# A linear-attention and two-MoE kernel: attention's stretches at other steps, block 0's input turned on TensorE, masks of five chunks on GpSimd

## The chip, the cores and the metric

One core of one Trainium2 chip. The time is the device time of one launch in microseconds (us), median of the runs; less is better.

## The reference

Three layers run one after the other on 3072 tokens of 384 features, all in f32:

```python
for t in range(S):                       # 4 batches, 8 heads, S = 768, head_dim 48
    state = alpha[:, :, t, :, None] * state + einsum('bhd,bhe->bhde', k[:, :, t], v[:, :, t])
    y[:, :, t] = einsum('bhd,bhde->bhe', q[:, :, t], state)
x = tokens(y)                            # 3072 x 384
x = square(relu(x @ w_in)) @ w_out       # 384 -> 2048 -> 384, f64 weights
logits = x @ w_gate + modality_bias[modality_id]
e = argmax(logits)                       # one of 8 experts per token
out = softmax(logits)[e] * (relu(x @ w1[e]) @ w2[e])   # 384 -> 1024 -> 384
```

## The kernel before

**Attention** is cut into 24 chunks of 128 tokens (u = 0 to 23, two batches in turns). For a chunk, `a_scan` and `a_scan2` form running products of alpha on VectorE (DVE) and scale k and q with them. `a_p` multiplies them on TensorE (PE) into two PSUM tiles pp of 128x512, and VectorE masks each half into the SBUF tile pt with one bitwise and. `a_kt` turns k, and ScalarE (ACT) copies it to kt. `a_y` multiplies v by pt, and the carried state by q, into py; ScalarE copies it to y, and two stores put it into the DRAM tensor yt_d, features by tokens. `a_state` multiplies kt by v and VectorE adds that to the state. `finish(u)` is a_y, a_state and, further on, the loads of chunk u + 2; `group(u)` is finish(u - 1), then a_p, a_kt and a_scale of u.

**The first MoE layer** goes over 12 blocks of 256 tokens (n), two chunks each, and 16 slices of 128 hidden features (f). One pair (n, f) is a step. `a_yload` loads a block's x from yt_d into xf, features by tokens, and `a_x` splits it: xh is x rounded on ScalarE, xl the rest on VectorE. Every product is made of three (high by high, high by low, low by high; `mm3`). A step's layer 1 is nine products of 128x256 into ph. ScalarE (relu into g) and VectorE (times relu again), or ScalarE twice in blocks 0 and 1, make the square; gh and gl are its split. Layer 2 comes three steps later (LAG1), six products of 128x392 into po. After a block's last step, VectorE forms lg, ScalarE copies one half of po to ob and VectorE the other; they free the PSUM for the next block's po.

**Weights.** `convert(f)` makes f32 out of f64 bits: per half, ScalarE's mag (line 276) and three rows on VectorE (279, 280, 281). `split` (259, 260) makes wh and wl. `gate_flip` turns w_out's slice on TensorE into pwt, in the one PSUM tile tagged "y", which py, and in a_p of chunks 4 to 6 the second pp, use too; `gate_columns` multiplies it by the gate's weights (306) and appends the result to wh and wl (307, 308).

**Order.** TensorE's instructions go in the order in which the program issues them. The other engines' queues are ordered when the program is built, and each runs its queue in order, as SP does with the DMAs. The program issues `early()` (chunks 0 to 2, the first weights) and then the list `seq` of steps: block 0 alone for 8 steps (LEAD), then blocks 0 and 1 in turns, 32 steps in all (`two`), then blocks 2 to 11. What else is issued stands in `at[gs]`, ahead of the step's layer 1. For block n, `g0` is its first step, and `GA` says at which of its steps the groups of chunks 2n + 3 and 2n + 4 stand. A group's a_scan is issued 4 steps ahead of it, its a_scan2 2 steps; the next block's a_yload stands at step 12, its a_x at 15. `spread` puts the routing of the block before (r_logits, r_rank, r_table) at the steps of ROUTE: 3, 5, 9, 10 to 14. `keep_warm` issues products of the constant tile delta whose result nobody reads.

**After that** come the experts' slots, which gather tokens by expert, on the same engines; GpSimd (POOL) issues their gathers and scatters.

Of the kernel before, what the change touches and what calls it, by code (L numbers as in the profile page):

```python
# [8 lines left out]
F32 = mybir.dt.float32  # L9
F32R = mybir.dt.float32r  # L10
BF16 = mybir.dt.bfloat16
I32 = mybir.dt.int32
AF = mybir.ActivationFunctionType
ALU = mybir.AluOpType
# [3 lines left out]
B, H, S, D = 4, 8, 768, 48  # L18
N = B * S
DM = H * D  # L20
# [3 lines left out]
C = 128  # L24
NU = N // C
CPB = S // C
HP = H // 2
HR = 112
TB = 256
NB = N // TB  # L30
ND = DM // 128
# [148 lines left out]
def gla_moe_moe2(ctx: ExitStack, tc: tile.TileContext, ain, vin, al_d, wio_d, wg_d, wgt_d, mid_d, mb_d, w12_d, out):  # L180
    nc = tc.nc
    pe, act, dve, pool, sp = nc.tensor, nc.scalar, nc.vector, nc.gpsimd, nc.sync
# [10 lines left out]
    p1 = mkpool("p1", 1)  # L193
    p2 = mkpool("p2", 2)
# [4 lines left out]
    ps2 = mkpool("ps2", 2, space=PSUM)  # L199
    ps1 = mkpool("ps1", 1, space=PSUM)  # L200
# [7 lines left out]
    mask = const.tile([128, C], I32, name="mask")  # L208
# [36 lines left out]
    def load_attn(u):  # L245
        load_al(u)
        load_qkv(u)
# [63 lines left out]
    un = {}  # L311
    xt = {}

    def a_scan(u):
        al, qk, v = attn_in.pop(u)
        q, k = qk[:, 0:HP * C], qk[:, HP * C:]
        ar3 = p2.tile([HR, HP, C + 1], F32, name="ar")
        ar = ar3.rearrange("p g t -> p (g t)")
        mul = dve if u < MULD else pool
        dve.tensor_tensor_scan(out=ar, data0=al[:, 0:HP * (C + 1)], data1=delta.rearrange("p g t -> p (g t)"), initial=0.0, op0=ALU.mult, op1=ALU.add)  # L320
        mul.tensor_tensor(out=k.rearrange("p (g t) -> p g t", g=HP), in0=k.rearrange("p (g t) -> p g t", g=HP), in1=ar3[:, :, 0:C], op=ALU.mult)
        ac = ar3[:, :, C:C + 1]

        inv = d1[:, 1:].rearrange("p (g t) -> p g t", g=HP)[:, :, C:]
        dve.tensor_scalar(out=inv, in0=ac, scalar1=PROD_MIN, scalar2=None, op0=ALU.max)
        dve.reciprocal(out=inv, in_=inv)
        un[u] = dict(q=q, k=k, v=v, ac=ac, al=al, mul=mul)
# [9 lines left out]
    def a_p(u):  # L337
        x = un[u]
        pp = [ps1.tile([128, HP, C], F32, tag=t, name="pp") if u in ATG else ps2.tile([128, HP, C], F32, tag="out" if u == 1 else "P", name="pp") for t in ("ms", "y")]
        for hp in range(HP):  # L340
            for j, (r0, r1) in enumerate(((0, 64), (64, HR))):
                pe.matmul(out=pp[j][:, hp, :], lhsT=x["k"][r0:r1, hp * C:(hp + 1) * C], rhs=x["q"][r0:r1, (HP - 1 - hp) * C:(HP - hp) * C], start=True, stop=True)
        x["pt"] = []
        for j in range(2):
            if u in (1, 3):
                pt = p3.tile([128, 2, XW], F32, tag="ob", name="pt").rearrange("p j d -> p (j d)")[:, 0:HP * C].rearrange("p (g t) -> p g t", g=HP)
            else:
                pt = p1.tile([128, HP, C], F32, tag=f"pt{j}", name="pt")
            dve.tensor_tensor(out=pt.bitcast(I32), in0=pp[j].bitcast(I32), in1=mask[:, None, :].to_broadcast([128, HP, C]), op=ALU.bitwise_and)
            x["pt"].append(pt)  # L350

    def a_kt(u):
        x = un[u]
        pk = ps1.tile([128, HP, HR], F32, tag="ms", name="pk")
        for hp in range(HP):
            pe.transpose(out=pk[:, hp, :], in_=x["k"][:, hp * C:(hp + 1) * C], identity=ident[0:HR, 0:HR])
        kt = p1.tile([128, HP, HR], F32, name="kt")
        act.copy(out=kt, in_=pk)
        x["kt"] = kt
# [6 lines left out]
    def a_state(u):  # L366
        x = un.pop(u)
        c = u // 2 % CPB
        if c == CPB - 1:
            return  # L370
        kv = ps1.tile([HR, HP, D], F32, tag="ms", name="kv")
        for hp in range(HP):
            for r0, r1 in ((0, 64), (64, HR)):
                pe.matmul(out=kv[r0:r1, hp, :], lhsT=x["kt"][:, hp, r0:r1], rhs=x["v"][:, hp, r0:r0 + D], start=True, stop=True)
        t = st_t[u % 2][:, :, 0:D]
        if c:
            dve.tensor_tensor(out=t, in0=t, in1=kv, op=ALU.add)
        else:
            dve.tensor_copy(out=t, in_=kv)

    def a_y(u):
        x = un[u]
        c = u // 2 % CPB

        py = ps1.tile([HR, HP, C], F32, tag="y", name="py")
        if c:
            for hp in range(HP):
                for r0, r1 in ((0, 64), (64, HR)):
                    pe.matmul(out=py[r0:r1, hp, :], lhsT=st_t[u % 2][r0:r1, hp, 0:r1 - r0], rhs=x["q"][r0:r1, (HP - 1 - hp) * C:(HP - hp) * C], start=not hp, stop=False, skip_group_check=True)  # L389
        for hp in range(HP):  # L390
            for j, (r0, r1) in enumerate(((0, 64), (64, HR))):
                pe.matmul(out=py[r0:r1, hp, :], lhsT=x["v"][:, hp, r0:r1], rhs=x["pt"][j][:, hp, :], start=not c and not hp, stop=True, skip_group_check=True)
        y = p1.tile([HR, HP, C], F32, name="y")
        act.copy(out=y, in_=py)
        yd = yt_d.rearrange("(g j e) t -> j e g t", g=HP, j=2)
        for j, (r0, r1) in enumerate(HRNG):
            sp.dma_start(out=yd[j, :, :, u * C:(u + 1) * C], in_=y[r0:r1])

    def a_yload(n):
        x = p1.tile([128, ND, TB], F32, name="xf")  # L400
        sp.dma_start(out=x, in_=yt_d.rearrange("(d p) t -> p d t", p=128)[:, :, n * TB:(n + 1) * TB])
        xt[n] = x

    def a_x(n):
        xh = p2.tile([128, ND, TB], F32R, name="xh")
        xl = p2.tile([128, ND, TB], F32R, name="xl")
        act.copy(out=xh, in_=xt[n])  # L407
        dve.tensor_tensor(out=xl, in0=xt[n], in1=xh, op=ALU.subtract)  # L408
        xt[n] = (xh, xl)

    def transpose_split(y, dst, j, pp, tag):
        px = pp.tile([128, ND, 128], F32, tag=tag, name="px")
        for d in range(ND):
            pe.transpose(out=px[:, d, :], in_=y[:, d * 128:(d + 1) * 128], identity=ident)
        hi, lo = (t[:, :, j * 128:(j + 1) * 128] for t in dst)
        act.copy(out=hi, in_=px)
        dve.tensor_tensor(out=lo, in0=px, in1=hi, op=ALU.subtract)
# [351 lines left out]
    ROUTE0 = 14, 15, 16, 17, 18, 19, 20, 21  # L769
    ROUTE = 3, 5, 9, 10, 11, 12, 13, 14  # L770
    ROUTEZ = 3, 3, 4, 5, 6, 6, 7, 8
    GA = 1, 8
    PRE = 4
    LEAD = 8
    LAG1 = 3
    POOLGL = ()
    WARM = 4
    MULD = NU

    ATG = {4: 12, 5: 18, 6: 24}  # L780
    gq = {}

    if True:
# [15 lines left out]
        def keep_warm(n):  # L799
            warm = ps2.tile([HR, HP * C], F32, tag="h", name="warm")  # L800
            for _ in range(n):
                pe.matmul(out=warm, lhsT=delta[:, 0, 0:HR], rhs=delta.rearrange("p g t -> p (g t)")[:, 0:HP * C], start=True, stop=True)
# [25 lines left out]
        def scan(u):  # L828
            a_scan(u)
            a_scan2(u)  # L830

        def finish(u, load=True):
            a_y(u)
            a_state(u)
            if load and u + 2 < NU:
                load_attn(u + 2)

        def group(u):

            finish(u - 1)  # L840
            if u < NU:
                a_p(u)
                a_kt(u)
                a_scale(u)
# [41 lines left out]
        def put(gs, *steps):  # L886
            at.setdefault(gs, []).extend(steps)

        def early():
            scan(0)  # L890
            a_p(0)
            a_kt(0)
            scan(1)
            finish(0, False)
            a_p(1)
            a_kt(1)
            a_scan(2)
            cv(0)
            a_scan2(2)
            cv(0)  # L900
            cv(0)
            finish(1, False)
            cv(0)
            cv(0)
            cv(1)
            a_yload(0)
            load_attn(3)
            cv(1, 3)
            cv(2)
            a_scale(2)  # L910
            gate_columns(*gate_flip())
            a_p(2)
            a_kt(2)
            a_x(0)

        put(1, lambda: finish(2, False), lambda: load_attn(4), lambda: a_scan(3))
        put(2, lambda: a_scan2(3), lambda: a_scale(3))
# [14 lines left out]
        for n in range(2, NB):  # L932
            g0 = two + (n - 2) * NF
            for i in range(2):
                u = 2 * n + 3 + i
                if u <= NU:
                    put(g0 + GA[i] + 2 * (u == 7), lambda u=u: group(u))
                    if u < NU:
                        put(g0 + GA[i] - 4, lambda u=u: a_scan(u))
                        put(g0 + GA[i] - 2, lambda u=u: a_scan2(u))  # L940
            if n < NB - 1:
                put(g0 + 12, lambda n=n: a_yload(n + 1))
                put(g0 + 15, lambda n=n: a_x(n + 1))
        g0 = two + (NB - 3) * NF
# [10 lines left out]
        for m in range(NB - 1):  # L955
# [7 lines left out]
            g0 = two + (m - 1) * NF  # L963
            spread([g0 + k for k in (ROUTE if 0 < m < NB - 2 else ROUTE0 if m == 0 else ROUTEZ)], route())
        for i in range(NA):
            g0 = two + (3 + i // 2) * NF + 8 * (i % 2)
# [157 lines left out]
```

## Time and profile before

| | |
|---|---|
| median of 3 runs | 825.29 us (824.69 to 828.78) |
| the profiled execution's own time | 822.23 us |
| its span, first to last instruction | 820.4 us |
| TensorE busy | 769.2 us, 94%, 6174 instructions |
| VectorE busy | 543.6 us, 66% |
| ScalarE busy | 402.6 us, 49% |
| GpSimd busy | 64.5 us, 8% |
| granted TensorE clock, mean | 0.974 of 2.4 GHz |
| DMA | 105.39 MB, 128 GB/s over the span |

Busy time is the union of an engine's instructions. A product of f32 tiles is two instructions in attention, and its end is modelled. A row of a timeline has the start in us from the span's start, the duration of the merged instructions, engine, line, operation, the tile written and those read, shapes and count; in brackets stands the idle time of the engine before it and what ended that. A row of waits sums such idle times. A granted clock of 1.00 is 2.4 GHz, 0.50 is 1.2 GHz.

### The profile page before, as it was taken

The numbers are of one execution on the slowest core, as the hardware profiler recorded it, in microseconds if no ns is written. First come the engines' busy times: TensorE is split into PE (matmuls) and PEld (weight loads), VectorE is DVE, ScalarE is ACT, GpSimd is POOL, SyncE is SP. The second block draws the span as 40 slices with busy tenths as digits, with TensorE's granted clock in tenths as the row PEclk, the third lists the DMA queues.
The fourth block names the chain that finished last, engine by engine and source line by source line (L and its number), as shares of the span: only waits on it lengthen the run. The fifth ranks groups of instructions, "written<-read, shape, count | busy, mean of one in ns | idle before, by whom it ended". The sixth has DMA issues, their size and how long they took to land. (4 is left out here: it accounts for less than half of the span.)

```text
span 820.4 us, 16492 instructions
## 1 busy us (share of the span) xinstructions
PE 769.2 (94%) x6174; PEld 738.6 (90%) x6174; DVE 543.6 (66%) x1370; ACT 402.6 (49%) x895; POOL 64.5 (8%) x85
## 2 busy tenths in 40 slices
PE   6589999999999999999999999999899999999992
PEld 4478989999998998999999999999889999999992
DVE  8889985776665664676767554456896666666631
ACT  2467879533333333333333333334666666666631
POOL 1000000000000000000000000002013322223110
PEclk9599999999999999999999999999999999999996
DMA  8877566232313211222222211105878777777600
GB/s 241 232 198 219 173 182 192 63 87 56 90 50 103 62 58 39 81 61 76 63 64 64 64 30 30 30 20 172 248 241 240 237 218 230 227 224 231 194 30 18
DMA packets 56019, 105.39 MB, mean 128 GB/s; under 512 B 9163, under 2 KB 29141, under 8 KB 55920
## 3 DMA queue, kind: packets, MB, share of 16 engines
q1 hardware_dynamic: 52720, 94.49, 39.2%
q0 software_dynamic: 3200, 9.65, 3.4%
q8 instruction: 53, 0.87, 0.5%
q14 instruction: 46, 0.38, 0.2%
HBM read 89.95 MB, written 14.36 MB: 127 GB/s over the span
## 5 line engine op out<-in xcount | busy, mean ns | idle before, releaser
L430 PE MATMUL ph<-xh,wh 128*128 128x256 f32 x864 | 249.7, 289 | 7.9 <-ACT xh L407 4.8
L430 PE MATMUL ph<-xl,wh 128*128 128x256 f32 x864 | 243.0, 281 | 1.5 <-DVE xl L408 1.5
L430 PE MATMUL ph<-xh,wl 128*128 128x256 f32 x864 | 243.0, 281 | 0.0
L430 PE MATMUL po<-wh,gh 128*128 128x392 f32 (+1 forms) x584 | 201.6, 345 | 9.4 <-ACT ob L874 5.7
L430 PE MATMUL po<-wh,gl 128*128 128x392 f32 (+1 forms) x584 | 198.3, 340 | 0.0
L430 PE MATMUL po<-wl,gh 128*128 128x392 f32 (+1 forms) x584 | 198.2, 339 | 0.0
L430 PEld LDWEIGHTS ph<-xh,wh 128*128 128x128 f32 x864 | 163.5, 189 | 10.9 <-ACT xh L407 5.1
L430 PEld LDWEIGHTS ph<-xl,wh 128*128 128x128 f32 x864 | 163.8, 190 | 1.8 <-DVE xl L408 1.8
L430 PEld LDWEIGHTS ph<-xh,wl 128*128 128x128 f32 x864 | 163.5, 189 | 0.0
L260 DVE TENSOR_TENSOR wl<-st,wh 128x768 fp32r<-128x768 f32 x104 | 99.5, 957 | 62.5 <-ACT wh L259 62.5
L996 ACT CAST gh<-g 128x256 fp32r<-128x256 f32 x192 | 77.9, 406 | 116.5 <-DVE g L992 116.1
L998 DVE TENSOR_TENSOR gl<-g,gh 128x256 fp32r<-128x256 f32 x192 | 80.8, 421 | 62.3 <-ACT gh L996 61.9
L430 PEld LDWEIGHTS po<-wh,gh 128*128 128x128 f32 x584 | 110.1, 189 | 11.5 <-ACT ob L874 6.9
L985 ACT ACTIVATE g<-ph 128x256 f32<-128x256 f32 x192 | 73.6, 383 | 94.9 <-PE ph L430 94.6
L259 ACT CAST wh<-st 128x768 fp32r<-128x768 f32 x104 | 86.7, 834 | 56.0 <-PE po L430 42.6
L992 DVE SCALAR_TENSOR_TENSOR g<-ph,g 128x256 f32<-128x256 f32 x160 | 67.3, 421 | 66.1 <-ACT g L985 65.7
L430 PEld LDWEIGHTS po<-wl,gh 128*128 128x128 f32 x584 | 110.3, 189 | 0.0
L430 PEld LDWEIGHTS po<-wh,gl 128*128 128x128 f32 x584 | 110.0, 188 | 0.2 <-DVE gl L998 0.2
L727 ACT ACTIVATE gh<-ph 128x256 fp32r<-128x256 f32 x96 | 37.0, 386 | 22.3 <-PE ph L430 20.3
L729 DVE SCALAR_TENSOR_TENSOR gl<-ph,gh 128x256 fp32r<-128x256 f32 x96 | 40.0, 417 | 8.6 <-ACT gh L727 8.5
L563 POOL IOTA row<- 1x96 f32 x1 | 0.2, 234 | 473.7 <-PE py L389 473.7
L745 POOL DMA_INDIRECT out_dram<-xs,ix x25 | 27.3, 1093 | 114.9 <-ACT xs L744 59.6
(187 smaller groups left out, 817.0 us busy)
## 6 DMA issues: line engine op xcount, KB each, us to landing
st<-in_w_dram SPq DMA_DIRECT2D x104, 384.0 KB, 3.9
st<-in_wio_dram SPq DMA_DIRECT2D x32, 384.0 KB, 4.0
qk<-in_ain_dram SPq DMA_DIRECT2D x23, 448.0 KB, 4.2
al<-in_ain_dram SPq DMA_DIRECT2D x24, 226.2 KB, 2.9
v<-in_vin_dram SPq DMA_DIRECT2D x24, 224.0 KB, 3.3
scr<-ob SPq DMA_DIRECT2D x12, 385.0 KB, 3.0
yt_d<-y SPq DMA_DIRECT2D x48, 96.0 KB, 2.8
xf<-yt_d SPq DMA_DIRECT2D x12, 384.0 KB, 3.5
```

Source lines behind the costliest of these rows:

```text
L259: act.copy(out=hi[:, 0:2 * DM], in_=t)
L260: lo_eng.tensor_tensor(out=lo[:, 0:2 * DM], in0=t, in1=hi[:, 0:2 * DM], op=ALU.subtract)
L430: pe.matmul(out=out_, lhsT=lhs[a][lsl], rhs=rhs[b][rsl], start=first and i == 0, stop=last and i == 2)
L563: pool.iota(thr, pattern=[[0, E], [SLOT, NJ]], base=0, channel_multiplier=0, allow_small_or_imprecise_dtypes=True)
L727: act.activation(out=gh[:, cols], in_=h, func=AF.Relu)
L729: dve.scalar_tensor_tensor(out=gl[:, cols], in0=h, scalar=0.0, in1=gh[:, cols], op0=ALU.max, op1=ALU.subtract)
L745: pool.indirect_dma_start(out=out[:, :], out_offset=bass.IndirectOffsetOnAxis(ap=x["ix"][:, 2 + j:3 + j], axis=0), in_=xo[:, 0:DM], in_off ...
L985: act.activation(out=g, in_=ph, func=AF.Relu)
L992: dve.scalar_tensor_tensor(out=g, in0=ph, scalar=0.0, in1=g, op0=ALU.max, op1=ALU.mult)
L996: act.copy(out=gh, in_=g)
L998: (pool if n in POOLGL else dve).tensor_tensor(out=gl, in0=g, in1=gh, op=ALU.subtract)
```

## The change

1. For chunks 2 to 6 (`PSEL`), ScalarE copies each half of pp from PSUM to pt, and GpSimd masks pt in place with an affine select. Chunks 0, 1 and 7 to 23 keep VectorE's mask.
2. Chunks 0 and 1 go through `a_first`: y is formed as tokens by features (eight products of 48 columns into pyt), ScalarE copies it to yt, and after a_state `transpose_split` turns it in three transposes into px and splits px into xh and xl of block 0 directly, 128 tokens each. px is taken from the two-buffer PSUM tag "out", which pp of chunk 1 uses too. The stores of y of these chunks, the load of xf and a_x for block 0 go.
3. `keep_warm` is issued with three products ahead of chunk 0's y and two ahead of chunk 1's, into the PSUM tag "h".
4. The groups stand at steps 3 and 10 of a block instead of 1 and 8 (chunk 7's stood at 3 already). The scans move with them.

```diff
@@ a_p
-            dve.tensor_tensor(out=pt.bitcast(I32), in0=pp[j].bitcast(I32), in1=mask[:, None, :].to_broadcast([128, HP, C]), op=ALU.bitwise_and)
+            if u in PSEL:
+                act.copy(out=pt, in_=pp[j])
+                pool.affine_select(out=pt, in_=pt, compare_op=ALU.is_ge, fill=0.0, base=-127, pattern=[[0, HP], [1, 128]], channel_multiplier=1)
+            else:
+                dve.tensor_tensor(out=pt.bitcast(I32), in0=pp[j].bitcast(I32), in1=mask[:, None, :].to_broadcast([128, HP, C]), op=ALU.bitwise_and)
...
+    def a_first(u):
+
+        x = un[u]
+        py = ps1.tile([128, DM], F32, tag="y", name="pyt")
+        for hp in range(HP):
+            for j in range(2):
+                o = (2 * hp + j) * D
+                pe.matmul(out=py[:, o:o + D], lhsT=x["pt"][j][:, hp, :], rhs=x["v"][:, hp, 64 * j:64 * j + D], start=not o, stop=True, skip_group_check=True)
+        y = p1.tile([128, DM], F32, tag="y", name="yt")
+        act.copy(out=y, in_=py)
+        if 0 not in xt:
+            xt[0] = tuple(p2.tile([128, ND, TB], F32R, name=k) for k in ("xh", "xl"))
+        return lambda: transpose_split(y, xt[0], u, ps2, "out")
...
-    GA = 1, 8
+    GA = 3, 10
...
+    PSEL = range(2, 7)
...
         def finish(u, load=True):
-            a_y(u)
+            turn = a_first(u) if u < 2 else a_y(u)
             a_state(u)
+            if turn:
+                turn()
...
             a_kt(0)
+            keep_warm(3)
             scan(1)
             finish(0, False)
             a_p(1)
             a_kt(1)
+            keep_warm(2)
...
-            a_yload(0)
             load_attn(3)
...
             a_kt(2)
-            a_x(0)
...
-                    put(g0 + GA[i] + 2 * (u == 7), lambda u=u: group(u))
+                    put(g0 + GA[i], lambda u=u: group(u))
```

**How it moves instructions.** A row has the line, the operation, the tile written and those read, the shape written, and a count. The changed kernel's lines are some 4 to 21 higher: 342 stays, 349 is 353, 392 of chunks 0 and 1 is replaced by 410 (pyt), 408 of block 0 by 432 (px) and 435 (xl).

The first place is TensorE between chunk 0's state and chunk 1's y; in brackets stand the engines and queues whose semaphores a row waits for (`DVE_49` is VectorE). Before:

```order
L374 MATMUL kv<-v,kt 48x48
L342 MATMUL pp<-qk 128x128 [waits DMAHW5_49]
L342 MATMUL pp<-qk 128x128 x7
L356 MATMUL pk<-ident,qk 128x112 [waits DVE_49]
L356 MATMUL pk<-ident,qk 128x112 x3
L392 MATMUL py<-pt,v 64x128 [waits DMAHW6_49,DVE_49,Activation_49]
```

Now:

```order
L378 MATMUL kv<-v,kt 48x48
L432 MATMUL px<-ident,yt 128x128 [waits Activation_49]
L432 MATMUL px<-ident,yt 128x128 x2
L342 MATMUL pp<-qk 128x128 [waits DMAHW5_49]
L342 MATMUL pp<-qk 128x128 [waits DVE_49]
L342 MATMUL pp<-qk 128x128 x6
L360 MATMUL pk<-ident,qk 128x112 x4
L821 MATMUL warm<-delta 112x512 x2
L410 MATMUL pyt<-v,pt 128x48 [waits DMAHW6_49,DVE_49]
```

The transposes of chunk 0 stand ahead of chunk 1's pp, whose second product waits for VectorE; two constants' products stand behind pk.

The second place is VectorE from the copy of chunk 0's state to chunk 1's mask. Before:

```order
L379 COPY state_105<-kv 112x4x48
L279 TENSOR_SCALAR w<-mag 128x384
L364 TENSOR_TENSOR state_105<-state_105,ar 112x4x48
L280 SCALAR_TENSOR_TENSOR w<-st,w 128x384
L279 TENSOR_SCALAR w<-mag 128x384
L349 TENSOR_TENSOR pt<-pp,mask 128x512 x2
```

Now:

```order
L279 TENSOR_SCALAR w<-mag 128x384
L280 SCALAR_TENSOR_TENSOR w<-st,w 128x384
L383 COPY state_105<-kv 112x4x48
L281 SCALAR_TENSOR_TENSOR w<-mag,w 128x384
L279 TENSOR_SCALAR w<-mag 128x384 x2
L280 SCALAR_TENSOR_TENSOR w<-st,w 128x384
L435 TENSOR_TENSOR xl<-px,xh 128x3x128
L281 SCALAR_TENSOR_TENSOR w<-mag,w 128x384
L280 SCALAR_TENSOR_TENSOR w<-st,w 128x384
L279 TENSOR_SCALAR w<-mag 128x384
L321 TENSOR_TENSOR qk<-qk,ar 112x512
L353 TENSOR_TENSOR pt<-pp,mask 128x512 x2
```

From the first of these rows on the mask stands behind twelve instructions, among them half of block 0's xl, where it stood behind five.

The third place is ScalarE where the steady block 5 begins, about the copy ob of block 4. Before:

```order
L394 COPY y<-py 112x512
L358 COPY kt<-pk 128x448
L985 ACTIVATE g<-ph 128x256
L996 CAST gh<-g 128x256
L985 ACTIVATE g<-ph 128x256
L996 CAST gh<-g 128x256
L874 COPY ob<-po 128x384
```

Now:

```order
L1017 CAST gh<-g 128x256
L895 COPY ob<-po 128x384
L398 COPY y<-py 112x512
L485 ACTIVATE ex<-sh 128x16
L362 COPY kt<-pk 128x448
L1006 ACTIVATE g<-ph 128x256
```

ob stood two steps behind the group's y and kt; now it stands ahead of y. Behind the second group of a block, xh (407, now 425) comes after y, kt and two pairs of g and gh in both kernels.

## Rows read from the trace of the kernel before

**Rows 1.** Windows: us, busy us (instructions) of PE PEld DVE ACT POOL, clock, DMA
```profile
20.00:43.00 23.00, 13.39 (x95) 11.34 (x92) 20.32 (x41) 9.71 (x20) 0.00 (x0) 0.57 0.76 219
...
64.00:130.00 66.00, 61.63 (x521) 58.50 (x521) 57.62 (x129) 52.53 (x132) 0.00 (x0) 1.00 0.62 189
130.00:440.00 310.00, 301.60 (x2628) 289.08 (x2627) 202.11 (x570) 122.74 (x308) 0.00 (x0) 1.00 0.26 75
```

**Rows 2.** TensorE's waits, whole run: line waited for, us in total, times, longest
```profile
PE po L430 <- ACT ob L874: 5.7, 6, 1.2
PE ph L430 <- ACT xh L407: 4.8, 1, 4.8
PE py L392 <- DVE pt L349: 3.4, 1, 3.4
...
PE ph L430 <- DVE g L992: 2.6, 3, 1.9
...
PE pwt L299 <- DVE pt L349: 2.4, 2, 1.6
...
PE ph L430 <- DVE xl L408: 1.5, 1, 1.5
...
PE pk L356 <- DVE pt L349: 0.5, 1, 0.5
```

**Rows 3.** Timeline of ScalarE, head: start, us, operation, [idle before <-releaser]
```profile
21.55 0.58 ACT L394 COPY y<-py 112x512 f32<-112x512 f32 x1
```

**Rows 4.** Timeline of TensorE, head (an f32 product is two instructions)
```profile
1.59 5.83 PE L802 MATMUL warm<-delta 112*112 112x512 f32 x8 [1.59 <-POOL delta L793]
...
36.48 0.84 PE L299 MATMUL pwt<-ident,w 128*128 128x128 f32 x3
```

**Rows 5.** Timeline of VectorE, head
```profile
16.31 0.33 DVE L379 COPY state<-kv 112x192 f32<-112x192 f32 x1
...
17.83 1.28 DVE L349 TENSOR_TENSOR pt<-pp,mask 128x512 int32<-128x512 int32 x2
...
25.59 0.62 DVE L279 TENSOR_SCALAR w<-mag 128x384 int32<-128x384 int32 x2
...
28.92 1.02 DVE L280 SCALAR_TENSOR_TENSOR w<-st,w 128x384 int32<-128x384 int32 x2
...
45.08 0.96 DVE L260 TENSOR_TENSOR wl<-w,wh 128x768 fp32r<-128x768 f32 x1 [0.15 <-ACT wh L259]
```

**Rows 6.** VectorE's waits from 16 to 60 us
```profile
DVE wl L308 <- ACT wh L307: 2.3, 4, 1.1
DVE state L377 <- PE kv L374: 1.0, 1, 1.0
DVE w L279 <- PE pwt L299: 0.7, 1, 0.7
```

**Rows 7.** Timeline of GpSimd, head
```profile
1.97 0.28 POOL L806 TENSOR_SCALAR_AFFINE_SELECT mkf<-mkf 128x128 f32<-128x128 f32 x1
```

**Rows 8.** Timeline of TensorE at the start and the middle of two blocks
```profile
300.38 1.09 PE L392 MATMUL py<-pt,v 128*64 128x128 f32 x16
...
369.13 1.08 PE L389 MATMUL py<-qk,state 64*64 64x128 f32 x16
...
373.08 0.37 PE L430 MATMUL ph<-xh,wh 128*128 128x256 f32 x1
...
377.42 0.28 PE L430 MATMUL ph<-xh,wh 128*128 128x256 f32 x1
...
379.56 0.44 PE L430 MATMUL po<-wh,gh 128*128 128x392 f32 x1 [0.90 <-ACT ob L874]
```

**Rows 9.** Timeline of the SP queue in the block of 300.38
```profile
307.20 0.38 SPq L401 DMA_DIRECT2D xf<-yt_d  x1
```

**Rows 10.** Timeline of VectorE in the same block
```profile
312.82 0.96 DVE L408 TENSOR_TENSOR xl<-xf,xh 128x768 fp32r<-128x768 f32 x1 [2.06 <-ACT xh L407]
```

**Rows 11.** The tile xf over the run: its loads
```profile
DMA to landing us min/median/max: 3.2/3.5/5.0
```

## The prediction

> **What bounds the kernel now.** I read the stretches first, then who waits for whom, and only then rows in order of time. TensorE is busy nearly throughout, so time is to be had only where it stands idle or runs at its lower clock, and the stretches tell where. From 130 to 440 us, the steady blocks, it is busy for 301.60 of 310 us and idle for 8.4. From 20 to 43 us, before and around the first step, it is busy for 13.39 of 23 us at a granted clock of 0.57, that is mostly at 1.2 GHz. From 64 to 130 us it idles for 4.4 us while VectorE is busy for 57.62 of 66 [rows 1]. The list of TensorE's waits names what ended the idle time: 5.7 us in six pieces for ob (the copy of a finished block's result, which frees its PSUM), 4.8 for xh and 1.5 for xl of block 0, 3.4 for chunk 0's mask [rows 2]. The reader should see that the head has two limits of nearly one height, TensorE's chain and VectorE's queue of weight conversions: what comes off one of them alone is lost to the other.
>
> **Head, TensorE's side.** Block 0's x goes by DRAM now: y of chunk 1 is copied at 21.55 in 0.58 us [rows 3], stored, loaded again and split, and the first step's products end at 36.48 [rows 4]. The change turns y on TensorE: one ScalarE copy, three transposes and two half splits in place of that. The waits for xh and xl go, 4.8 + 1.5 = 6.3 us [rows 2]. On the SP queue four stores and a load go too, and chunk 3's loads no longer stand behind stores that wait for y.
>
> Three things are added or moved. *The constants' products.* Four took 5.83 us at the start [rows 4], 1.46 each, so three take at most 4.4, 1.0 more than the 3.4 us wait for chunk 0's mask that they fill, and less at the upper clock; two lie in the wait for chunk 1's. I book nothing, and up to 1.0 in the lower end. *A new wait.* px of chunk 0 takes one of the two PSUM buffers that chunk 1's pp use, so its second pp product stands until VectorE has made xl from px, behind six conversion rows and the state copy: some 4 us, which pk and py of chunk 1 wait with it. *A moved mask.* Chunk 1's mask began at 17.83, 1.5 us after the state copy at 16.31 [rows 5]. Ahead of it stand now four L279 (two take 0.62), five L280 or L281 (two take 1.02), the state copy of 0.33, a multiply (0.64, as half a mask) and half an xl (0.48, as half a wl) [rows 5]: 1.24 + 2.55 + 1.45 = 5.2 us, so it begins near 21.5, and the new wait is over by then. TensorE therefore comes to step 0 near 28, not much later than it reaches its wait now, and starts it at once: the products end between 28.5 (at 2.4 GHz) and 33 (if it stays at 1.2) instead of 36.48. This chain gains 3.5 to 8 us.
>
> **Head, VectorE's side.** It sets the end here, since each step needs wl of its weights. The fourth step's wl starts at 45.08 [rows 5]. On the way VectorE waits 4.0 us for TensorE's late chain (2.3 behind wh, 1.0 for kv, 0.7 for pwt) [rows 6]; these go if x is early. The masks of chunks 2 and 3 leave it, 1.28 us each [rows 5]. The two half xl cost what the whole one did. That is 6.6 us. Against it I put 1.5 us of new waits of VectorE for kv, px and xh of chunk 1, which TensorE now makes later. **Head: 5 us**, between 1.5 and 8.5.
>
> What hides the masks' new cost: per chunk two ScalarE copies of 0.58, as y's [rows 3], and two GpSimd selections. One of 128x128 took 0.28 [rows 7]; one of 128x512 lies between that and four times it, 1.12. I take 0.85, nearer the upper end since it passes over four times the elements. Chunk 2's pt is then there 2.9 us after pp, while TensorE still has pk, step 0, a turn of gate weights and the state's half of py to do. If ScalarE comes late, py stands, and layer 1 of the next step behind it.
>
> **64 to 130 us.** The gate weights' turn waits 2.4 us for the masks of chunks 4 and 5, whose pp lie in its PSUM bank, and pk 0.5 for chunk 6's [rows 2]. ScalarE's copies free the bank now, behind other ScalarE work and 1.2 us for the pair. I take half, **1.5 us**, with bounds of 0 and 2.9.
>
> **The blocks.** A step takes 2.17 us (two from 373.08 to 377.42), the group of attention ahead of it began at 369.13, so it takes 4.0; then the new block's first layer 2 waits 0.90 for ob at 379.56 [rows 8]. The group stood at step 1 and is over by then. At step 3 it stands between the old block's last layer 2 and the new block's first, and ob is copied under it. **All six waits go, 5.7 us** [rows 2]; the least I would believe is 4. What is late next is y: the second group stands at step 10 instead of 8 and writes the y that the next block loads. In one block that load was issued at 307.20 [rows 9], and xl stood in VectorE's queue for 2.06 us before xh came [rows 10]; TensorE's 1.9 us for g [rows 2] are that case. ScalarE's order keeps xh behind the second relu after the group, as before, so the distance stays and I book nothing more for it.
>
> **Sum.** 5 + 1.5 + 5.7 = 12.2 us. The profiled execution took 822.23 us for a span of 820.4. It lies 3.1 below the median of 825.29, so the sum gives 810 on its time and **813 us** on the median, which I predict. All lower ends (1.5 - 1.0 + 0 + 4) leave 821, all upper ends (8.5 + 2.9 + 5.7, and 1.9 for the late load) 806.
>
> **Rivals.**
> *GpSimd holds VectorE up.* GpSimd's rows before 440 us are its set-up [rows 7], so no row shows it at work beside VectorE's scans and splits: the trace neither bears this out nor excludes it. If every selection stops VectorE for its length, chunks 2 and 3 cost 4 x 0.85 = 3.4 us in the head, and the gain at chunks 4 to 6 goes: 5 - 3.4 + 0 + 5.7 = 7.3, so 818 us. The Trainium skill, "SBUF — State Buffer", section "SBUF: two separate sides", says this of the pair: a GpSimd instruction and a VectorE one that reads two inputs from SBUF exclude each other, and the one that comes second stands for the whole length of the first. Chance 0.15.
> *The waits for ob come back as waits for g.* At step 3 the group's scan, mask and state meet the routing's rows on VectorE; g comes late, and ph with it. Against it: the group crowds VectorE as much at step 1 now, and there are only three waits for g in the whole run [rows 2]. If all 5.7 come back, 6.5 are left: 819 us. Chance 0.08.
> *The x load comes too late in every block, and the kernel is slower.* After a group, 4.0 us, TensorE runs four steps, 8.7, before the layer 1 that needs the PSUM which the g behind xl frees: 12.7. Back from there, g takes 0.4, xl 0.95 and xh about as much, so the load must have landed 10.4 us after the group began. In the row shown it was issued 6.8 us after (300.38 to 307.20 [rows 8, 9]), and loads take 3.2 to 5.0 [rows 11]: 10 to 11.8. Each us beyond is paid in nine blocks. The 12.2 us are eaten where all nine land at 11.8; at 12.7 the stall is 2.3 each, 20.7 in all: 834 us. Against it: one such stall of 1.9 us now, and the order keeps the distance. Chance 0.05.
>
> **How the numbers follow.** Forecast 0.72, the rivals 0.15, 0.08 and 0.05. A measurement of this kernel tells 0.5%, 4.1 us, from no change, so the line is at 821.2. The forecast lies below it but for its farthest end, 818 and 819 do by less than their own spread: faster 0.87, same 0.09, slower 0.04. The range of 805 to 820 holds the forecast, the 818 and the 819, and leaves out the last rival and the far lower end.
>
> **What would show it.** Right: no wait of po for ob; none for xh or xl before step 0, whose products end before 33 us; the fourth wl near 40; GpSimd selections under 1.2 us. Wrong: VectorE rows that stretch while those run; xl standing over 1 us in VectorE's queue in most blocks; py waiting for pt of chunks 2 to 6; conversions waiting for weights, whose transfers run at 219 GB/s in the head already [rows 1].

## The result, and the profile after

The changed kernel takes **815.47 us** (median of 6 runs, 812.33 to 817.51) against 824.99 for the kernel before beside it (6 runs, 822.40 to 828.78): ratio 0.9873, 95% interval 0.9846 to 0.9900. The forecast was 813 us, its range 805 to 820. The profiled execution took 815.84 us for a span of 814.1 at a mean granted clock of 0.976; before it was 822.23 for 820.4 at 0.974.

The stretches of the changed kernel, to be read against [rows 1]: us, then busy us and instructions of PE, PEld, DVE, ACT, POOL, then granted clock, DMA share and GB/s.

```profile
0.00:20.00 20.00, 15.30 (x77) 8.30 (x79) 16.70 (x32) 5.05 (x9) 2.91 (x20) 0.95 0.87 238
20.00:43.00 23.00, 20.07 (x162) 16.44 (x160) 17.37 (x36) 10.93 (x24) 1.62 (x2) 0.74 0.76 207
43.00:60.00 17.00, 13.12 (x93) 12.01 (x92) 14.62 (x31) 12.15 (x30) 1.54 (x2) 0.87 0.71 181
64.00:130.00 66.00, 60.60 (x493) 56.96 (x491) 56.39 (x126) 51.85 (x128) 6.10 (x4) 0.99 0.62 183
130.00:440.00 310.00, 308.70 (x2723) 297.48 (x2718) 211.62 (x591) 129.36 (x324) 1.23 (x2) 1.00 0.27 77
```

In the steady blocks, 130 to 440 us, TensorE is idle for 1.3 us where it was for 8.4. In the head TensorE is busier than before and VectorE less busy (17.37 of 23 us against 20.32): VectorE now stands. From 64 to 130 us TensorE idles for 5.4 us instead of 4.4, so nothing came of the 1.5 us forecast there.

TensorE's waits over the whole run, which answer to [rows 2]:

```profile
PE pwt L306 <- ACT wt L301: 4.3, 6, 1.2
PE pwt L299 <- DVE w L281: 2.9, 3, 1.4
PE pp L342 <- DVE xl L435: 2.6, 1, 2.6
PE pwt L299 <- DVE wl L308: 1.9, 3, 0.7
...
PE ph L448 <- DVE wl L260: 1.4, 2, 1.1
PE ph L448 <- DVE g L1013: 1.3, 2, 0.7
```

The 5.7 us for ob, the 4.8 for xh and the 1.5 for xl of block 0 are gone, the 3.4 for chunk 0's mask fell to 0.5 and the 2.6 for g to 1.3. New is pp for xl, once, 2.6 us (px holds its PSUM buffer). The waits of the gate weights' turn grew: for w from 0.4 to 2.9, for wt from 2.5 to 4.3.

To see which part brought what, I compare the starts of the same instruction in both traces. Chunk 5's y (its first product of q and the state) starts at 125.87 us before and at **129.70** in the changed kernel: up to there the changed kernel is 3.8 us behind in these two executions, where 6.5 of gain were forecast. From there to layer 1 of step 170 (the first is step 0) it takes 389.6 us instead of 399.0: the blocks have won **9.4**, where 5.7 were forecast. So the sum came out near because two errors had opposite signs, and that is luck.

The head's chain on TensorE in the changed kernel, to be read against [rows 4]: start, us, operation, [idle before it <- who ended that].

```profile
15.85 0.55 PE L432 MATMUL px<-ident,yt 128*128 128x128 f32 x3
16.32 0.49 PE L342 MATMUL pp<-qk 64*128 64x128 f32 x2
19.40 2.07 PE L342 MATMUL pp<-qk 48*128 48x128 f32 x14 [2.59 <-DVE xl L435]
21.40 1.01 PE L360 MATMUL pk<-ident,qk 112*128 112x112 f32 x4
22.20 3.24 PE L821 MATMUL warm<-delta 112*112 112x512 f32 x4
25.27 1.88 PE L410 MATMUL pyt<-v,pt 128*128 128x48 f32 x16
...
31.51 0.36 PE L448 MATMUL ph<-xh,wh 128*128 128x256 f32 x1
```

The first step starts at 31.51 instead of near 28. VectorE's side of it, against [rows 5, 6]:

```profile
21.09 1.29 DVE L353 TENSOR_TENSOR pt<-pp,mask 128x512 int32<-128x512 int32 x2
...
27.81 0.36 DVE L383 COPY state<-kv 112x192 f32<-112x192 f32 x1 [3.02 <-PE kv L378]
...
41.00 0.35 DVE L381 TENSOR_TENSOR state<-state,kv 112x192 f32<-112x192 f32 x1 [1.99 <-PE kv L378]
...
45.38 0.96 DVE L260 TENSOR_TENSOR wl<-w,wh 128x768 fp32r<-128x768 f32 x1
```

Chunk 1's mask begins at 21.09, as worked out (21.5). But after it VectorE stands 3.02 and 1.99 us for kv of chunks 1 and 2, and the fourth step's wl starts at 45.38, as late as before (45.08) and not near 40.

### The profile page after: what moved, and what is told of

It reads as the page before. It is cut to its first block, busy times and chain, and to the rows that moved or that the text cites. A ratio compares the mean times of both kernels' runs of the same rounds, so it can differ in the third digit from the quotient of the medians.

```text
span 814.1 us, 16533 instructions
## 1 busy us (share of the span) xinstructions
PE 776.7 (95%) x6190; PEld 742.9 (91%) x6190; DVE 545.3 (67%) x1361; ACT 408.3 (50%) x906; POOL 73.3 (9%) x95
## 5 line engine op out<-in xcount | busy, mean ns | idle before, releaser
L701 POOL DMA_INDIRECT xs<-scr,ix x25 | 28.4, 1137 | 70.5 <-DVE rf L521 21.7
```

The source lines that it names most:

```text
L701: pool.indirect_dma_start(out=xs[:, j, 0:XW], out_offset=None, in_=scr[0:rows, :], in_offset=bass.IndirectOffsetOnAxis(ap=ix[:, j:j + 1], ...
```

## The experiments

The times stand together here. Clock (granted, mean from 0 to 60 us), first step and chunk 5's y are those of each profiled execution, in us.

```
kernel                               median (runs)       ratio to before [95%]   clock  step 0  chunk 5's y
before (first profile)               825.29 (3)                                  0.80   32.52   125.87
changed                              815.47 (6)          0.9873 [0.9846 0.9900]  0.85   31.51   129.70
1 stretches at steps 3, 10 alone     815.28 (6)          0.9870 [0.9843 0.9897]  0.80   32.35   126.01
2 all but the stretches              822.04 (12)         0.9975 [0.9954 0.9996]  0.91   30.75   127.50
3 masks on VectorE                   814.38 (6)          0.9886 [0.9858 0.9915]  0.89   30.46   126.22
4 px in other buffers                811.36 (5)          0.9835 [0.9808 0.9862]  0.97   26.98   121.82
5 no added products                  815.87 (9)          0.9917 [0.9892 0.9942]  0.77   33.31   129.05
6 x by DRAM                          816.85 (6)          0.9917 [0.9888 0.9946]  0.89   31.64   126.68
7 px in other buffers, no products   815.71 (6)          0.9906 [0.9876 0.9935]  0.74   34.04   130.40
8 px in other buffers, masks VectorE 813.28 (6)          0.9889 [0.9854 0.9924]  0.92   27.17   126.62
9 wait for px filled                 811.10 (6)          0.9846 [0.9817 0.9876]  0.97   29.87   123.88
10 as 4, again                       811.98 (6)          0.9836 [0.9806 0.9867]  0.91   29.27   125.02
11 as 8, again                       815.52 (6)          0.9897 [0.9869 0.9924]  0.83   31.60   128.20
```

The kernel before, beside them, took 823.86 (1 to 4), 824.27 (5 to 8) and 823.81 (9 to 11). One kernel's head moves by some 3 us between executions (4 and 10: 121.82 and 125.02), so the medians decide where two traces are that close. The changed kernel ran beside a kernel before of 824.99, about 1 us more; where medians and ratios tell different things of it, both are given.

### 1 and 2. The stretches alone, and all the rest alone

On the kernel before:

```diff
-    GA = 1, 8
+    GA = 3, 10
...
-                    put(g0 + GA[i] + 2 * (u == 7), lambda u=u: group(u))
+                    put(g0 + GA[i], lambda u=u: group(u))
```

> The kernel before with the groups at steps 3 and 10 alone; the head is the old one. Theory A (from the changed kernel's trace: its head is 3.8 us late at chunk 5's y, 129.70 against 125.87, and the blocks win more than that back): the blocks alone bring 8 to 10 us, ratio 0.988 to 0.990, chunk 5's y within 1 us of 125.87, no wait of po for ob. Theory B (the forecast: 5.7 us from the blocks, the rest from the head): 5 to 6.5 us, ratio 0.992 to 0.994.

The other kernel undoes these lines in the changed kernel.

> The changed kernel with the groups back at steps 1 and 8: all of the head's edits and GpSimd's masks, none of the blocks'. Theory A: no gain, 0 to 4 us slower than before (ratio 1.000 to 1.005), chunk 5's y near 129, the six waits for ob back at 5 to 6 us. Theory B: 5 to 6.5 us faster, ratio 0.992 to 0.994.

The stretches alone take 815.28 us, the whole change's time, 8.6 us less than before, as theory A had it (the ratio, 0.9870, is a little under its 0.988), with chunk 5's y at 126.01. Their blocks, from the windows:

```profile
130.00:440.00 310.00, 308.09 (x2686) 297.09 (x2686) 212.91 (x592) 126.19 (x318) 0.00 (x0) 1.00 0.27 76
```

and no wait for ob is left. Without the stretches it stands there as before; this is the first row of TensorE's waits in the second kernel:

```profile
PE po L448 <- ACT ob L895: 5.7, 6, 1.3
```

That kernel's ratio is 0.9975, a gain of 0.3 to 3.8 us. Neither expectation of its time was met: theory A had it 0 to 4 us slower, with chunk 5's y near 129 (it came at 127.50), theory B 5 to 6.5 faster. So the head's three parts together are worth little (2 us alone, nothing measurable beside the stretches), though the waits that they were to take away are gone. The next runs ask which part loses what another gains.

### 3. The masks of chunks 2 to 6 back on VectorE

```diff
-    PSEL = range(2, 7)
+    PSEL = ()
```

> The changed kernel with the masks of chunks 2 to 6 back on VectorE. Theory A with a lock between GpSimd and VectorE (in the changed kernel VectorE rows of usually 0.55 us take 0.89 to 0.99 beside the selections): the masks' move is worth little, so within 2 us of the changed kernel either way, ratio to the kernel before 0.985 to 0.991. Theory B (the masks' 2.5 us on VectorE and 1.5 us of pwt's waits are a gain): 3 to 4 us slower than the changed kernel, ratio 0.991 to 0.993.

814.38 us, within theory A's 2 us of the changed kernel: the masks' move is worth nothing that can be measured here. TensorE's turn of the gate weights waits longer without it (5.1 us for w against 2.9, and 2.0 for masks), and yet chunk 5's y comes 3.5 us earlier in this execution, at a higher clock.

### 4. px in other PSUM buffers

```diff
-        return lambda: transpose_split(y, xt[0], u, ps2, "out")
+        return lambda: transpose_split(y, xt[0], u, ps2, "h")
```

> The changed kernel with px of chunks 0 and 1 in the PSUM tag h instead of out, so that chunk 1's pp needn't wait for VectorE's xl. If that wait (2.6 us) and the late, slow-clocked products behind it (pyt and kv of chunk 1 end at 27.8) are what cost the head its gain, the wait of pp goes, step 0 starts 3 us or more before 31.5, chunk 5's y comes at 126 or earlier, and the time falls by 3 to 5 us against the changed kernel (ratio to before 0.982 to 0.984). If the head's end is set later, by conversions on VectorE from 44 us on, step 0 comes earlier but chunk 5's y stays within 1.5 us of 129.7 and the time within 1.5 us of the changed kernel's.

811.36 us, by the medians 4.1 less than the changed kernel, by the ratios 3.1; the expectation was met in each point. Its chain on TensorE, to be held against that of the changed kernel above:

```profile
15.69 0.55 PE L432 MATMUL px<-ident,yt 128*128 128x128 f32 x3
16.16 1.16 PE L342 MATMUL pp<-qk 64*128 64x128 f32 x16
17.30 0.60 PE L360 MATMUL pk<-ident,qk 112*128 112x112 f32 x4
17.74 1.88 PE L821 MATMUL warm<-delta 112*112 112x512 f32 x4
...
26.98 0.56 PE L448 MATMUL ph<-xh,wh 128*128 128x256 f32 x1
```

From the start of chunk 1's pp to the first step it takes 10.8 us instead of 15.2, 4.4 less, more than the wait of 2.59. The rest is in the durations: pp and pk take 1.14 + 0.44 us here, start to start, and 5.08 - 2.59 + 0.80 in the changed kernel without its wait; the two constants' products 2.10 (a wait of 0.22 for the mask included) against 3.07. Of these gains 0.9 is lost again between y and the first step. So in these two executions the wait cost its length and then the clock. Two things changed at once, though: the products come earlier, and they run faster.

### 5 and 7. Without the added constants' products

```diff
-            keep_warm(3)
...
-            keep_warm(2)
```

once on the changed kernel, once with px in the other buffers.

> The changed kernel without its five added constants' products; all else as changed. In the changed kernel's profile the two before y of chunk 1 stand from 22.20 to 25.27 us, 3.08 at 1.2 GHz, while chunk 1's mask began at 21.09 and takes 1.28: some 2.9 of the 3.08 us lie on the path to the first step. Theory (px's wait for its PSUM buffer cost the head its gain, the products only lengthen it): the 2.6 us wait of pp for xl stays, the first step starts 2 to 3 us earlier than 31.51, chunk 5's y near 128 instead of 129.7, time 812.5 to 815. Rival (the products keep the clock up, and without them it is lower for longer): granted clock from 20 to 43 us under 0.70, the first step no earlier, 816 to 819. Second rival (the products were the whole loss): as fast as the kernel with px in the other buffer, 811.

> The changed kernel with px in the other PSUM buffers and without the five added constants' products. Theory (with px's wait gone the masks' waits are all that the products fill, and they keep the clock up there): first step between 26 and 28 us, the granted clock from 20 to 43 us below the 0.93 of the kernel with the products, time 811 to 814 against 811.4. Rival (the products stand on the path in this version too, 1 to 2 us ahead of each y): first step near 25, 809 to 810.5.

In the changed kernel the products do little for the time: 815.87 without them against 815.47; by the ratios 0.0044, 3.6 us, with intervals that overlap. My theory missed there (first step at 33.31, not 2 to 3 us earlier), and the rival that they keep the clock up came near: a clock of 0.57 from 20 to 43 us, the first step no earlier, a time 0.1 under its range. Without them the wait for px is short, since TensorE is late already:

```profile
12.79 3.82 PE L410 MATMUL pyt<-v,pt 128*128 128x48 f32 x16 [2.93 <-DVE pt L353]
...
19.63 2.07 PE L342 MATMUL pp<-qk 48*128 48x128 f32 x14 [0.44 <-DVE xl L435]
```

Its clock is 0.50 from 12.4 to 36.2 us, so there was no upper clock left that a wait could end.

With px in the other buffers the products do count: 815.71 without, 811.4 and 812.0 with. The first step comes at 34.04 there, and the granted clock from 20 to 43 us is 0.50, that is 1.2 GHz throughout. Of that kernel, TensorE in the head:

```profile
12.86 0.42 PE L410 MATMUL pyt<-v,pt 128*128 128x48 f32 x2 [3.13 <-DVE pt L353]
...
20.99 3.82 PE L410 MATMUL pyt<-v,pt 128*128 128x48 f32 x16
24.74 1.09 PE L378 MATMUL kv<-v,kt 128*64 128x48 f32 x16
```

y takes 3.82 us here and 1.88 in the changed kernel's chain. My expectation, first step at 26 to 28 and 811 to 814 us, missed: the clock stays low for longer than I had thought. So the free buffer brings nothing without the products (815.87 and 815.71), and the products little while px holds the buffer: **each is needed for the other's full worth**. That leaves two readings of the wait: it makes TensorE late, or it undoes what the products are there for.

### 9. The wait for px filled, not removed

On the changed kernel, px in the buffer as changed:

```diff
             finish(0, False)
+            keep_warm(3)
             a_p(1)
```

> The changed kernel, px in the buffer as changed, with three more constants' products on TensorE ahead of chunk 1's pp: they fill the wait for px's PSUM buffer (2.59 us, three products take 2.3 at 2.4 GHz) without taking it away. Theory (the wait costs twice: its own 2.6 us, and the lower clock from 18.1 to 24.9 us that follows the idle time): clock stays up, so pk, the products, y and kv of chunk 1 take 6.6 us less the half that the clock gives back; first step between 28 and 29.8 us instead of 31.51 (26.98 with px in the other buffer), time 812 to 815. Rival (only the lateness counts): first step at 31 to 32, 815 to 817.

811.10 us, all that the other buffer brings by the medians (the ratios, 0.9846 and 0.9873, lie 2.2 us apart and their intervals just touch). The time is under the theory's 812 to 815, and the first step at 29.87, only 1.6 us earlier than in the changed kernel, just misses its 28 to 29.8. Chunk 1's pp still comes late:

```profile
15.79 0.55 PE L432 MATMUL px<-ident,yt 128*128 128x128 f32 x3
16.18 2.74 PE L821 MATMUL warm<-delta 112*112 112x512 f32 x6
18.84 1.65 PE L342 MATMUL pp<-qk 64*128 64x128 f32 x16
20.43 0.60 PE L360 MATMUL pk<-ident,qk 112*128 112x112 f32 x4
20.86 1.88 PE L821 MATMUL warm<-delta 112*112 112x512 f32 x4
```

The stretch from 18.2 to 24.8 us shows what changed: first the changed kernel, then this one.

```profile
18.20:24.80 6.60, 5.40 (x22) 3.55 (x23) 6.59 (x13) 2.13 (x4) 0.00 (x0) 0.50 0.94 258
```

```profile
18.20:24.80 6.60, 5.94 (x37) 3.52 (x35) 6.60 (x14) 2.58 (x5) 0.00 (x0) 1.00 0.88 259
```

The granted clock is 0.50 in the one and 1.00 in the other, and TensorE has 22 instructions in it against 37. The rival, that only the lateness counts (815 to 817 us, first step at 31 to 32), falls. VectorE's 3.02 us for kv fell to 0.8 in this kernel.

Two things limit this. Of the 5.8 us by which chunk 5's y is earlier, 4.2 come behind the first step (the clock from 43 to 60 us is 1.00 against 0.87), and no run shows that they follow from the filled wait. And the clock isn't set by the wait alone: from 18.2 to 24.8 us it is 0.50, 0.74 and 0.74 in the profiles with the wait (changed, 2, 3), 1.00, 1.00, 1.00 and 0.90 in four with the products and that wait gone or filled (4, 8, 9, 10), but 0.50 in experiment 11, which has the products and no wait for px. That the difference isn't of these executions alone is told by the mean granted clock of whole runs: its median is 0.978 for the changed kernel, 0.984 and 0.984 for experiments 4 and 10, 0.987 for 9, 0.973 and 0.975 without the products (5 and 7).

### 6. x of chunks 0 and 1 by DRAM

```diff
-            turn = a_first(u) if u < 2 else a_y(u)
+            turn = a_y(u)
...
+            a_yload(0)
...
+            a_x(0)
```

on the changed kernel; products, masks and stretches stay.

> The changed kernel with the x of chunks 0 and 1 by DRAM as before; the masks on GpSimd, the constants' products and the stretches at steps 3 and 10 stay. Theory (turning x on TensorE as written costs the head): the waits of ph for xh and xl come back, some 6 us less 1 for the products, but no wait of pp for xl; chunk 5's y within 1 us of 125.87 as in the kernel before, time 813 to 816, that is within 2 us of the changed kernel either way. Rival (the masks on GpSimd or the products are what holds the head up): chunk 5's y at 128 or later again though x goes by DRAM, 816 to 819.

816.85 us lies in the rival's range (816 to 819), not in the theory's 813 to 816, though within its 2 us of the changed kernel; chunk 5's y at 126.68 is where the theory put it (within 1 us of 125.87). Neither is shown. So turning x on TensorE as the change does it is worth 1.4 us by the medians and 3.6 by the ratios, whose intervals overlap. With the buffer free it is worth some 5 (811.4 against 816.85).

### 8, 10 and 11. The masks once more, with px in the other buffers

Experiment 4 with the edit of experiment 3, then both again side by side.

> The changed kernel with px in the other PSUM buffers and the masks of chunks 2 to 6 on VectorE, as before. Theory (what VectorE saves by the masks it loses again beside GpSimd's selections, as where px waited: 814.4 against 815.5): 810 to 812.5, within 1.5 us of the version with the masks on GpSimd; the waits of the gate weights' turn for w and for the masks come back, and VectorE's rows no longer stretch. Rival (with TensorE early, VectorE alone limits the head, and two masks of 1.28 us are worth their 2.6 us): 813.5 to 815, chunk 5's y 2 us later than 121.8.

> The changed kernel with px in the other PSUM buffers, once more, beside its sister with the masks on VectorE on the same chip. Before: 811.36, ratio 0.9835. Expected 810 to 813, first step within 0.3 us of 26.98.

> The same with the masks of chunks 2 to 6 on VectorE, once more. Theory (with TensorE early VectorE limits the head, so the masks that GpSimd takes off it count): 1.5 to 4 us more than its sister, chunk 5's y some 4 us later. Rival (the difference of 1.9 us between the medians was the spread of the runs): within 1.5 us of its sister.

Eleven runs with the masks on GpSimd have a median of 811.5 us (808.2 to 813.0), twelve with them on VectorE 815.1 (811.4 to 818.6). So the move is worth some 3.5 us here, where it was worth nothing in experiment 3: my first expectation (within 1.5 us) fell. Experiment 8 by itself, 1.9 us over experiment 4, lay between it and the rival; experiment 11, 3.5 over 10, bears the rival out. The first step of the repeated run (29.27, not 26.98) missed its expectation: the chain is the same to 23.6 us but for 0.4 us of lateness, then TensorE runs at the lower clock in this execution (pp of chunk 2 takes 2.08 us, in the other 1.16). How much of the 3.5 us is VectorE's time and how much the clock, which is 0.92 and 0.83 in these two profiles against 0.97 and 0.91, stays open.

The same runs say one thing more of the free buffer: with the masks on VectorE it brings nothing, 815.1 us against 814.38 where px holds it (experiment 3). Only with the masks on GpSimd does it bring 4 (811.5 against 815.47). So what comes off TensorE alone, or off VectorE alone, is lost, as the prediction says of the head's two limits.

## Why the prediction was near, and what was wrong in it

**The blocks: right in mechanism, too small.** All six waits for ob went, by the move that the prediction named [rows 2, 8]; in the block of 379.56 the new block's first layer 2 now follows the step's layer 1 at once, in the changed kernel's trace of TensorE:

```profile
375.39 0.28 PE L448 MATMUL ph<-xh,wl 128*128 128x256 f32 x1
375.51 0.34 PE L448 MATMUL po<-wh,gh 128*128 128x392 f32 x1
```

The term of 5.7 us measured 8.8 (stretches alone) to 9.4. Two things had been booked at nothing. The stall for the late x load [rows 2, 10] shrank: TensorE's waits for g in the blocks are 1.4 and 1.3 us against 2.2. And the blocks got shorter by more than their idle time: sixteen steps that held one wait of 0.90 us for ob took 43.87 us before (353.86 to 397.73) and 42.70 with the stretches moved, 1.17 less. Idle time fell by 6.5 to 7.1 us in all, the other 2.3 are of this kind. Not all of that is the wait's: the block before that starts at 454.68 held no wait, and its sixteen steps still took 42.88, 0.18 more than with the stretches moved. Where that 0.18 lies stays open.

**The head: the step that failed.** "[T]he new wait is over by then. TensorE therefore comes to step 0 near 28". The wait was seen, its place and end were right (mask at 21.5, measured 21.09), and it was shorter than the 4 us put down. What failed is that its cost was taken for its length, hidden behind the mask. Afterwards the clock was at 1.2 GHz, and what the wait had let slip had to be done at half the speed: the rest of pp, pk and the products (y and kv, 1.88 and 0.67 us, ran at 2.4 GHz again). The prediction gave both ends, 28.5 "at 2.4 GHz" and 33 at 1.2, and took the gain of 5 from VectorE's side without asking which of the two it was. The products end at 32.65, so the mark "before 33" was met by a chain that had nearly lost its gain. The wait has this price only while the masks are on GpSimd; with them on VectorE taking it away brings nothing (814.38 and 815.1 us).

The term "1.5 us of new waits of VectorE for kv, px and xh" is where this shows: kv alone was 3.02 + 1.99 = 5.0 us. That takes 3.5 of the 5 us. In the profile TensorE then loses more, behind conversions (waits for w, wl and wt) that are as late as before; in the medians the head is left with 0 to 2 us. Nothing came of the 1.5 us from 64 to 130 us: the waits for masks fell, and waits for conversions took their place. With px in the other buffers the term does come: TensorE is idle there for 3.7 and 4.0 us with the masks on GpSimd (experiments 4, 10), for 5.4 and 5.4 with them on VectorE (8, 11).

**Constants' products: booked at nothing, with the wrong reason.** They were weighed as length in two waits, and in the changed kernel they were worth little. But the clock is higher with them, and they are worth 4 us where the wait for px doesn't follow them (experiments 4, 7). The Trainium skill, "TensorE: Matmul & The Clock Gate", section "HAM oscillation — how this bites in real kernels", tells of waits after which TensorE starts each piece at the lower clock. The trace agrees: the stretch of 0.50 from 18.2 us on begins within the wait of 2.59 us.

**Rivals.** GpSimd does hold VectorE up, by the mechanism that this rival named, but for less than half of its price (3.5 us for ten selections, see the last section). Whether it cost the head some of its gain isn't isolated: experiment 3 takes it away together with the masks' move, and the time stays the same. Its selections take 0.6 to 1.0 us where 0.85 was taken, but 2.0 in one place, over the 1.2 named as a mark. The waits for g did not come back. xl stands longer in VectorE's queue than before (8 waits, 6.9 us, for xh), which the prediction named as a sign of the third rival, but TensorE stood for 1.3 us in all: the sign was badly chosen. Why a wait of 2.30 us there cost TensorE 0.5 us and one of 2.06 cost 1.9 before stays open.

**The best version** has px in the tag "h", or the wait filled: 811.1 to 812.0 us, 1.6% less than before and by the medians 4 us less than the change.

## What to carry to other kernels

Price a new TensorE wait in a head like this twice: by its length, and by what runs at half the clock behind it; give a temporary its own PSUM buffer, or put idle products into the wait. Look for edits that are worth little apart: here the free buffer with the products, and the free buffer with the masks on GpSimd. And when a total comes out near, compare the same instruction's start in both traces, stage by stage, before calling the working right.

## What the runs showed of the hardware

**VectorE rows that come upon a GpSimd selection stand until it ends.** GpSimd's rows in the changed kernel, two selections of 128x512 each:

```profile
31.89 1.62 POOL L351 TENSOR_SCALAR_AFFINE_SELECT pt<-pt 128x512 f32<-128x512 f32 x2 [28.32 <-DVE w L280]
49.08 1.54 POOL L351 TENSOR_SCALAR_AFFINE_SELECT pt<-pt 128x512 f32<-128x512 f32 x2 [15.56 <-ACT pt L350]
97.92 4.04 POOL L351 TENSOR_SCALAR_AFFINE_SELECT pt<-pt 128x512 f32<-128x512 f32 x2 [47.30 <-ACT pt L350]
120.03 2.06 POOL L351 TENSOR_SCALAR_AFFINE_SELECT pt<-pt 128x512 f32<-128x512 f32 x2 [18.07 <-ACT pt L350]
140.14 1.23 POOL L351 TENSOR_SCALAR_AFFINE_SELECT pt<-pt 128x512 f32<-128x512 f32 x2 [18.06 <-ACT pt L350]
```

One takes 0.6 us in the last pair and up to 2.0 beside a busy VectorE, as means of a pair; with x by DRAM (experiment 6) a pair takes up to 5.1. VectorE's rows at the ends of four of these pairs:

```profile
32.95 0.98 DVE L280 SCALAR_TENSOR_TENSOR w<-st,w 128x384 int32<-128x384 int32 x1
...
50.05 0.79 DVE L279 TENSOR_SCALAR w<-mag 128x384 int32<-128x384 int32 x1
...
101.46 0.91 DVE L280 SCALAR_TENSOR_TENSOR w<-st,w 128x384 int32<-128x384 int32 x1
...
121.51 0.60 DVE L325 TENSOR_SCALAR d<-ar 112x4 f32<-112x4 f32 x1
```

Their usual lengths are 0.55, 0.35, 0.55 and 0.17 us. Each ends 0.14 to 0.15 us before the end of the pair plus its own usual length: the third pair ends at 101.96, the row at 102.37, and 101.96 + 0.55 is 102.51. The other way round, a selection waits as well: these four pairs end 0.50 us behind the end of a VectorE row (at 33.02, 50.12, 101.46 and 121.59), and a selection of the last pair takes 0.64. By line, min/median/max in ns: the changed kernel, then the one with the masks on VectorE.

```profile
L280 DVE SCALAR_TENSOR_TENSOR w<-st,w x32: 528/552/981, 16.6 to 111.4; 128x384 int32<-128x384 int32 x32
```

```profile
L280 DVE SCALAR_TENSOR_TENSOR w<-st,w x32: 528/552/559, 16.6 to 109.8; 128x384 int32<-128x384 int32 x32
```

Only rows beside a selection are stretched: nine, by 0.25 to 0.44 us each, 3.5 us in all for ten selections, against the 6.4 us of masks that left VectorE. They include rows with one input from SBUF (279 and 325). Not every row stands: one of 0.17 us at 140.17 (m from sc), within the last pair's first selection, took its usual length. The Trainium skill, "SBUF — State Buffer", section "SBUF: two separate sides", has the second of the two stand for the whole instruction. The rows agree, but for the 0.14 us. Six of the nine lost 0.42 to 0.44 us because they came with 0.57 to 0.58 us of the selection left.

**The same program's clock differs between executions.** Experiments 4 and 10 are one kernel; their clock from 20 to 43 us is 0.93 and 0.78, and their first steps are 2.3 us apart. A head like this can't be judged by one profile.
